# A fused linear-attention and ELU-MLP kernel on one core: filler on constant data in the opening, narrower W_in pieces, another bank for one slice, and the first q load ahead of the iota

## The chip, the core and the metric

The kernel runs on one core of a Trainium2 chip. The core has TensorE (PE, with its weight loads shown as PEld), VectorE (DVE), ScalarE (ACT), GpSimd (POOL) and SyncE (SP). The metric is the device time of one execution in microseconds (us); the time before is the median of eight runs. Lower is better.

## The reference

Two stages follow each other. The first is causal linear attention with a decay `lam` per head, over 4 batches, 8 heads, 768 positions and a head dimension of 64, in blocks of positions with a state carried from block to block:

```python
intra = einsum('bhij,bhjd->bhid', (qb @ kb.T) * Dmask, vb)   # Dmask = lam ** (i - j), i >= j
inter = einsum('bhid,bhde->bhie', qb * lam_pow, kv_state)
out[:, :, block] = intra + inter
kv_state = lam_block * kv_state + einsum('bhsd,bhse->bhde', kb_decayed, vb)
```

The second takes the result as `x`, 3072 tokens of 512 values, and computes

```python
h = x @ w_in                                       # 512 -> 2048
g = where(h > 0, h, exp(min(h, 0)) - 1)            # ELU
out = g @ w_out                                    # 2048 -> 512
```

## The kernel before, in words

**Groups and token tiles.** The kernel works with blocks of 128 positions. A group `g` is one block of one batch: 6 blocks by 4 batches make 24 groups, and groups 0 to 3 are the first block of each batch. The 24 groups are put together to token tiles `t` of 4, 2, 4, 4, 4, 4 and 2 groups (`TS`), so tile 0 is groups 0 to 3 with 512 tokens.

**Attention of a group.** q and k are transposed (`att_T`, lines 207 to 224, by TensorE with an identity as the other operand, into tiles `psTq`, `psTk` or `psT`; later groups by a DMA, `att_xT`) and copied to SBUF (`att_Te`, ScalarE). `att_S` makes the scores (`psS`), `att_mask` multiplies them by the decay mask (VectorE, L320), `att_O` multiplies by v and adds the part that comes from the state (`psO`), and `att_X` writes the result to `xt`. `att_kd` (L295) makes the decayed k, for groups 0 to 3 on GpSimd; `att_U` and `att_st` update the state.

**The MLP of a token tile.** W_in is cut into 16 slices of 128 columns. `mm1` multiplies slice `n` of W_in (L441, or L459 for the tiles of two groups) with `xt` into a PSUM tile `psH`. ScalarE takes its exp (`e`, L470) and its relu (`r`, L474), and VectorE joins them to `g` (L487). For slices 2, 4 and 6 of tile 0 there is no relu and VectorE does two steps (L482, L485). `mm2` (L538) multiplies `g` by W_out into `psM`, which is copied out and stored. The last group's output is made in two parts (`mm2_last`).

**PSUM.** There are three tags, "S", "M" and "H", with two buffers each. A tile with a tag waits for the readers of the tile two before it with the same tag. `psH` has the tag "H", but in tile 0 the even slices below 8 have "M", which `psM` and the filler also use.

**Order.** Nothing is scheduled by a planner: the order of the program on each engine is written out by hand in the list `steps` and in `run`, which hangs functions on steps. Steps `('A', n)` are slice `n` of tile 0; steps `('B', n)` are the rest of the second matmul of tile 0, in between which group 4's transposes stand (step `('B', 1)`). From step `(1, 0)` on, token tile 1 and later ones follow.

**Loads.** All loads of q, k, v, W_in and W_out convert from float32 to float16 and are issued by GpSimd (POOL) in the order of the list `LOADS`, L72 for q, k and v, L97 for W_in (`emit_wi`), L104 for W_out (`emit_wo`). Entries `(g, n, 'q')` load `n` groups; `('wi', i)` and `('wo', i)` load piece `i`; `('kd', g)` is no load but the computation of the decayed k on GpSimd, at this place of its order. The pieces have the widths of `WI = [1, 1, 2, 2, 2, 4, 4]` slices and `WO = [2, 2, 4, 4, 4]`. The first twelve entries are q and k of groups 0 to 3, then v; W_in follows. From the entry that loads group 8 on, loads hang on steps and are paced (`paced_load`) by a one-element copy on GpSimd that reads a finished `g`. The small load of `lam` is on SyncE.

**The opening.** GpSimd makes `rel_i` by an iota (L127) before the first load. From it VectorE makes `rel`, the identity `ident16` (L140), the causal mask, `pos`, `row` and the lag, and clears the states `st` (L156). ScalarE makes `loglam`, `dn`, and the masks (`build_mask0`, L170). Meanwhile `warm(k)` (L560 to 568) lets TensorE run `k` filler matmuls into a PSUM tile `psW` that nobody reads; their operand on both sides is `ident16`. The list `W` says how many stand ahead of each step of the opening: `W[0]` ahead of group 0's q transposes, `W[1]` ahead of its k transposes, and so on to the first slice of the MLP.

The code that the change touches:

Of the kernel before, what the change touches and what calls it, by code (L numbers as in the profile page):

```python
# [8 lines left out]
FP16 = mybir.dt.float16  # L9
# [6 lines left out]
def kernel(  # L16
# [27 lines left out]
    cpool = ctx.enter_context(tc.tile_pool(name="cst", bufs=1))  # L44
# [16 lines left out]
    def emit_load(g, n=1, which="qkv"):  # L61
        c, b = divmod(g, B)
        rows = slice(c * L, (c + 1) * L)
        i, o = (g // 2) % NB, (g % 2) * H
        for w, src in (("q", q), ("k", k), ("v", v)):
            if w not in which:
                continue
            if w == "v":
                dst = vn[i][:, o : o + n * H, :]
            else:  # L70
                dst = (qn if w == "q" else kn)[i][:, o : o + n * H, :]
            nc.gpsimd.dma_start(  # L72
                out=dst, in_=src[b : b + n, :, rows].rearrange("b h p d -> p (b h) d")
            )
# [7 lines left out]

    WI = [1, 1, 2, 2, 2, 4, 4]
    WO = [2, 2, 4, 4, 4]
    wi_t, wo_t, wi_at, wo_at = [], [], {}, {}
    for i, w in enumerate(WI):
        for j in range(w):
# [7 lines left out]
    def emit_wi(i):  # L95
        f0 = sum(WI[:i]) * 128
        nc.gpsimd.dma_start(  # L97
            out=wi_t[i][:],
            in_=moe_w_in[:, f0 : f0 + WI[i] * 128].rearrange("(k p) f -> p k f", p=128),
        )  # L100

    def emit_wo(i):
        f0 = sum(WO[:i]) * 128
        nc.gpsimd.dma_start(  # L104
            out=wo_t[i][:],
            in_=moe_w_out[f0 : f0 + WO[i] * 128, :].rearrange("(n p) f -> p n f", p=128),
        )
# [4 lines left out]
    ]  # L112
    LOADS = [(0, 1, 'q'), (0, 1, 'k'), (1, 1, 'q'), (1, 1, 'k'), (2, 1, 'q'), (2, 1, 'k'), (3, 1, 'q'), (3, 1, 'k'), (0, 1, 'v'), (1, 1, 'v'), (2, 1, 'v'), (3, 1, 'v'), ('wi', 0), ('wi', 1), ('wi', 2), ('wi', 3), ('kd', 0), ('wi', 4), ('wi', 5), ('kd', 2), ('wo', 0), ('wi', 6), ('wo', 1), ('wo', 2), (4, 2), ('wo', 3), ('wo', 4), (6, 2), (8, 2), (10, 2), (12, 2), (14, 2), (16, 2), (18, 2), (20, 2), (22, 2)]

    def run_loads(items):
        for it in items:
            if it[0] == "wi":
                emit_wi(it[1])
            elif it[0] == "wo":
                emit_wo(it[1])  # L120
            elif it[0] == "kd":
                att_kd(it[1], 2, "p")
            else:
                emit_load(*it)

    run_loads(LOADS[:0])
    nc.gpsimd.iota(rel_i[:], pattern=[[1, 128]], base=0, channel_multiplier=-1)  # L127
    run_loads(LOADS[0:16])

# [6 lines left out]
    ident16 = cpool.tile([128, 128], FP16, name="ident16")  # L136
# [47 lines left out]
    def late_ks():  # L184
        nc.scalar.activation(ks[:], loglam[:], AF.Exp, scale=pos[:, 1:2])
# [15 lines left out]
    qT, kT, Pt, kds, xt, pT, pS = {}, {}, {}, {}, {}, {}, {}  # L201
# [230 lines left out]
    def mm1_mm(t, n, lo, hi, tag="H"):  # L432

        if n == 0 and lo == 0:
            gt[t] = msb.tile([128, NF, TS[t] * L], FP16, tag="g", bufs=2, name=f"g{t}")
        if lo == 0:
            pH_of[t, n] = ps.tile([128, TS[t] * L], FP32, tag=tag, bufs=2, name=f"psH{t}_{n}")
        pH = pH_of[t, n]
        wi, j = wi_t[wi_at[n][0]], wi_at[n][1]
        for kk in range(HP):  # L440
            nc.tensor.matmul(  # L441
                pH[:, lo:hi], lhsT=wi[:, kk, j * 128 : (j + 1) * 128],
                rhs=xt[t][:, kk, lo:hi], start=(kk == 0), stop=(kk == HP - 1),
            )

    def mm1(t, n, alt=False):

        MT = TS[t] * L
        if MT == 256:
            if n == 0:  # L450
                gt[t] = msb.tile([128, NF, MT], FP16, tag="g", bufs=2, name=f"g{t}")
            pH = ps.tile(
                [128, 2 * MT], FP32, tag="M" if (t, n) in ((1, 0),) else "H", bufs=2,
                name=f"psH{t}_{n}",
            )
            for x in range(2):
                wi, j = wi_t[wi_at[n + x][0]], wi_at[n + x][1]
                for kk in range(HP):
                    nc.tensor.matmul(  # L459
                        pH[:, x * MT : (x + 1) * MT],  # L460
                        lhsT=wi[:, kk, j * 128 : (j + 1) * 128],
                        rhs=xt[t][:, kk, :], start=(kk == 0), stop=(kk == HP - 1),
                    )
            MT *= 2
        else:
            if (t, n) not in pH_of:
                mm1_mm(t, n, 0, MT, "M" if t == 0 and n % 2 == 0 and n < 8 else "H")
            pH = pH_of.pop((t, n))
        e = msb.tile([128, MT], FP32, tag="e", bufs=3, name=f"e{t}_{n}")
        nc.scalar.activation(e[:], pH[:], AF.Exp)  # L470
        if alt:
            return e, None, pH
        r = msb.tile([128, MT], FP16, tag="r", bufs=3, name=f"r{t}_{n}")
        nc.scalar.activation(r[:], pH[:], AF.Relu)  # L474
        return e, r, pH
# [84 lines left out]
    def warm(k, tag="M"):  # L560
        if k <= 0:
            return
        pw = ps.tile([128, 4, 128], FP32, tag=tag, bufs=2, name=f"psW{len(warms)}")
        warms.append(pw)
        for _ in range(k):
            nc.tensor.matmul(  # L566
                pw[:, 0:2], lhsT=ident16[:], rhs=any16[:, 0:2], start=True, stop=True
            )

    warms = []  # L570
    pace = cpool.tile([1, 1], FP16, name="pace")
    any16 = ident16[:].unsqueeze(1).broadcast_to([128, 4, 128])

# [33 lines left out]
    op_T(2, "q")  # L607
    op_Te(2, "q")
    att_S(1)
    att_mask(1, 2)  # L610
    warm(W[5])
    op_T(2, "k")
# [31 lines left out]

    run_loads(LOADS[16:28])
    for s, g in zip([], (0, 2)):
# [35 lines left out]
    def paced_load(s, items):  # L682

        t, n = s
        if t not in ("A", "B"):
            w = 2 if TS[t] == 2 else 1
            src = gt[t][0:1, n - w, 0:1] if n else gt[t - 1][0:1, NF - 1, 0:1]
            nc.gpsimd.tensor_copy(pace[:], src)  # L688
        run_loads(items)

    for s, a, b in [(('B', 2), 28, 29), ((1, 2), 29, 30), ((1, 14), 30, 31), ((2, 4), 31, 32), ((2, 12), 32, 33), ((3, 4), 33, 34), ((3, 12), 34, 35), ((4, 4), 35, 36)]:
        at(s, paced_load, s, LOADS[a:b])

    steps = [(('A', 0), (0, 0), []), (('A', 1), (0, 1), []), (('A', 2), (0, 2), []), (('A', 3), (0, 3), []), (('A', 4), (0, 4), []), (('A', 5), (0, 5), []), (('A', 6), (0, 6), []), (('A', 7), (0, 7), []), (('A', 8), (0, 8), []), (('A', 9), (0, 9), []), (('A', 10), (0, 10), [(0, 0, 0), (0, 1, 0)]), (('A', 11), (0, 11), [(0, 0, 1), (0, 1, 1)]), (('A', 12), (0, 12), [(0, 0, 2), (0, 1, 2)]), (('A', 13), (0, 13), [(0, 0, 3), (0, 1, 3)]), (('A', 14), (0, 14), [(0, 0, 4), (0, 1, 4)]), (('A', 15), (0, 15), [(0, 0, 5), (0, 1, 5)]), (('B', 0), None, [(0, 2, 0), (0, 2, 1), (0, 2, 2), (0, 2, 3)]), (('B', 1), None, [(0, 2, 4), (0, 2, 5), (0, 3, 0), (0, 3, 1)]), (('B', 2), None, [(0, 3, 2), (0, 3, 3), (0, 3, 4), (0, 3, 5)]), (('B', 3), None, [(0, 0, 6), (0, 1, 6), (0, 2, 6), (0, 3, 6)]), (('B', 4), None, [(0, 0, 7), (0, 1, 7), (0, 2, 7), (0, 3, 7)]), (('B', 5), None, [(0, 0, 8), (0, 1, 8), (0, 2, 8), (0, 3, 8)]), (('B', 6), None, [(0, 0, 9), (0, 1, 9), (0, 2, 9), (0, 3, 9)]), (('B', 7), None, [(0, 0, 10), (0, 1, 10), (0, 2, 10), (0, 3, 10)]), (('B', 8), None, [(0, 0, 11), (0, 1, 11), (0, 2, 11), (0, 3, 11)]), (('B', 9), None, [(0, 0, 12), (0, 1, 12), (0, 0, 13), (0, 1, 13)]), (('B', 10), None, [(0, 0, 14), (0, 1, 14), (0, 0, 15), (0, 1, 15)]), (('B', 11), None, [(0, 2, 12), (0, 3, 12), (0, 2, 13), (0, 3, 13)]), (('B', 12), None, [(0, 2, 14), (0, 3, 14), (0, 2, 15), (0, 3, 15)]), ((1, 0), (1, 0), []), ((1, 2), (1, 2), []), ((1, 4), (1, 4), []), ((1, 6), (1, 6), [(1, 0, 0), (1, 1, 0), (1, 0, 1), (1, 1, 1)]), ((1, 8), (1, 8), [(1, 0, 2), (1, 1, 2), (1, 0, 3), (1, 1, 3)]), ((1, 10), (1, 10), [(1, 0, 4), (1, 1, 4), (1, 0, 5), (1, 1, 5)]), ((1, 12), (1, 12), [(1, 0, 6), (1, 1, 6), (1, 0, 7), (1, 1, 7)]), ((1, 14), (1, 14), [(1, 0, 8), (1, 1, 8), (1, 0, 9), (1, 1, 9)]), ((2, 0), (2, 0), [(1, 0, 10), (1, 0, 11)]), ((2, 1), (2, 1), [(1, 0, 12), (1, 0, 13)]), ((2, 2), (2, 2), [(1, 0, 14), (1, 0, 15), (1, 1, 10)]), ((2, 3), (2, 3), [(1, 1, 11), (1, 1, 12)]), ((2, 4), (2, 4), [(1, 1, 13), (1, 1, 14)]), ((2, 5), (2, 5), [(1, 1, 15), (2, 0, 0), (2, 0, 1)]), ((2, 6), (2, 6), [(2, 0, 2), (2, 0, 3)]), ((2, 7), (2, 7), [(2, 0, 4)]), ((2, 8), (2, 8), [(2, 0, 5), (2, 1, 0)]), ((2, 9), (2, 9), [(2, 0, 6), (2, 1, 1)]), ((2, 10), (2, 10), [(2, 0, 7), (2, 1, 2)]), ((2, 11), (2, 11), [(2, 0, 8), (2, 1, 3)]), ((2, 12), (2, 12), [(2, 0, 9), (2, 1, 4)]), ((2, 13), (2, 13), [(2, 0, 10), (2, 1, 5)]), ((2, 14), (2, 14), [(2, 0, 11), (2, 1, 6)]), ((2, 15), (2, 15), [(2, 0, 12), (2, 1, 7)]), ((3, 0), (3, 0), [(2, 0, 13), (2, 1, 8), (2, 0, 14), (2, 1, 9)]), ((3, 1), (3, 1), [(2, 0, 15), (2, 1, 10), (2, 1, 11), (2, 1, 12)]), ((3, 2), (3, 2), [(2, 1, 13), (2, 1, 14), (2, 1, 15), (2, 2, 0)]), ((3, 3), (3, 3), [(2, 2, 1), (2, 2, 2), (2, 2, 3), (2, 2, 4), (2, 2, 5)]), ((3, 4), (3, 4), [(2, 2, 6), (2, 2, 7), (2, 2, 8), (2, 2, 9)]), ((3, 5), (3, 5), [(2, 2, 10), (2, 2, 11), (2, 2, 12), (2, 2, 13)]), ((3, 6), (3, 6), [(2, 2, 14), (2, 2, 15), (2, 3, 0), (2, 3, 1), (2, 3, 2)]), ((3, 7), (3, 7), [(2, 3, 3), (2, 3, 4), (2, 3, 5), (2, 3, 6)]), ((3, 8), (3, 8), [(2, 3, 7), (2, 3, 8), (2, 3, 9), (2, 3, 10)]), ((3, 9), (3, 9), [(2, 3, 11), (2, 3, 12), (2, 3, 13), (2, 3, 14), (2, 3, 15)]), ((3, 10), (3, 10), [(3, 0, 0), (3, 0, 1), (3, 0, 2), (3, 0, 3)]), ((3, 11), (3, 11), [(3, 0, 4), (3, 0, 5), (3, 1, 0), (3, 0, 6)]), ((3, 12), (3, 12), [(3, 1, 1), (3, 0, 7), (3, 1, 2), (3, 0, 8), (3, 1, 3)]), ((3, 13), (3, 13), [(3, 0, 9), (3, 1, 4), (3, 0, 10), (3, 1, 5)]), ((3, 14), (3, 14), [(3, 0, 11), (3, 1, 6)]), ((3, 15), (3, 15), [(3, 0, 12), (3, 1, 7)]), ((4, 0), (4, 0), [(3, 0, 13), (3, 1, 8), (3, 0, 14), (3, 1, 9)]), ((4, 1), (4, 1), [(3, 0, 15), (3, 1, 10), (3, 1, 11), (3, 1, 12)]), ((4, 2), (4, 2), [(3, 1, 13), (3, 1, 14), (3, 1, 15), (3, 2, 0)]), ((4, 3), (4, 3), [(3, 2, 1), (3, 2, 2), (3, 2, 3), (3, 2, 4), (3, 2, 5)]), ((4, 4), (4, 4), [(3, 2, 6), (3, 2, 7), (3, 2, 8), (3, 2, 9)]), ((4, 5), (4, 5), [(3, 2, 10), (3, 2, 11), (3, 2, 12), (3, 2, 13)]), ((4, 6), (4, 6), [(3, 2, 14), (3, 2, 15), (3, 3, 0), (3, 3, 1), (3, 3, 2)]), ((4, 7), (4, 7), [(3, 3, 3), (3, 3, 4), (3, 3, 5), (3, 3, 6)]), ((4, 8), (4, 8), [(3, 3, 7), (3, 3, 8), (3, 3, 9), (3, 3, 10)]), ((4, 9), (4, 9), [(3, 3, 11), (3, 3, 12), (3, 3, 13), (3, 3, 14), (3, 3, 15)]), ((4, 10), (4, 10), [(4, 0, 0), (4, 0, 1), (4, 0, 2), (4, 0, 3)]), ((4, 11), (4, 11), [(4, 0, 4), (4, 0, 5), (4, 1, 0), (4, 0, 6)]), ((4, 12), (4, 12), [(4, 1, 1), (4, 0, 7), (4, 1, 2), (4, 0, 8), (4, 1, 3)]), ((4, 13), (4, 13), [(4, 0, 9), (4, 1, 4), (4, 0, 10), (4, 1, 5)]), ((4, 14), (4, 14), [(4, 0, 11), (4, 1, 6)]), ((4, 15), (4, 15), [(4, 0, 12), (4, 1, 7)]), ((5, 0), (5, 0), [(4, 0, 13), (4, 1, 8), (4, 0, 14), (4, 1, 9)]), ((5, 1), (5, 1), [(4, 0, 15), (4, 1, 10), (4, 1, 11), (4, 1, 12)]), ((5, 2), (5, 2), [(4, 1, 13), (4, 1, 14), (4, 1, 15), (4, 2, 0)]), ((5, 3), (5, 3), [(4, 2, 1), (4, 2, 2), (4, 2, 3), (4, 2, 4), (4, 2, 5)]), ((5, 4), (5, 4), [(4, 2, 6), (4, 2, 7), (4, 2, 8), (4, 2, 9)]), ((5, 5), (5, 5), [(4, 2, 10), (4, 2, 11), (4, 2, 12), (4, 2, 13)]), ((5, 6), (5, 6), [(4, 2, 14), (4, 2, 15), (4, 3, 0), (4, 3, 1), (4, 3, 2)]), ((5, 7), (5, 7), [(4, 3, 3), (4, 3, 4), (4, 3, 5), (4, 3, 6)]), ((5, 8), (5, 8), [(4, 3, 7), (4, 3, 8), (4, 3, 9), (4, 3, 10)]), ((5, 9), (5, 9), [(4, 3, 11), (4, 3, 12), (4, 3, 13), (4, 3, 14), (4, 3, 15)]), ((5, 10), (5, 10), [(5, 0, 0), (5, 0, 1), (5, 0, 2), (5, 0, 3)]), ((5, 11), (5, 11), [(5, 0, 4), (5, 0, 5), (5, 1, 0), (5, 0, 6)]), ((5, 12), (5, 12), [(5, 1, 1), (5, 0, 7), (5, 1, 2), (5, 0, 8), (5, 1, 3)]), ((5, 13), (5, 13), [(5, 0, 9), (5, 1, 4), (5, 0, 10), (5, 1, 5)]), ((5, 14), (5, 14), [(5, 0, 11), (5, 1, 6)]), ((5, 15), (5, 15), [(5, 0, 12), (5, 1, 7)]), ((6, 0), (6, 0), [(5, 0, 13), (5, 1, 8), (5, 0, 14), (5, 1, 9), (5, 0, 15)]), ((6, 2), (6, 2), [(5, 1, 10), (5, 1, 11), (5, 1, 12), (5, 1, 13), (5, 1, 14)]), ((6, 4), (6, 4), [(5, 1, 15), (5, 2, 0), (5, 2, 1), (5, 2, 2), (5, 2, 3), (5, 2, 4)]), ((6, 6), (6, 6), [(5, 2, 5), (5, 2, 6), (5, 2, 7), (5, 2, 8), (5, 2, 9)]), ((6, 8), (6, 8), [(5, 2, 10), (5, 2, 11), (5, 2, 12), (5, 2, 13), (5, 2, 14)]), ((6, 10), (6, 10), [(5, 2, 15), (5, 3, 0), (5, 3, 1), (5, 3, 2), (5, 3, 3), (5, 3, 4)]), ((6, 12), (6, 12), [(5, 3, 5), (5, 3, 6), (5, 3, 7), (5, 3, 8), (5, 3, 9)]), ((6, 14), (6, 14), [(5, 3, 10), (5, 3, 11), (5, 3, 12), (5, 3, 13), (5, 3, 14), (5, 3, 15)]), (('E', 0), None, [(6, 0, 0), (6, 0, 1), (6, 0, 2), (6, 0, 3), (6, 0, 4), (6, 0, 5), (6, 0, 6), (6, 0, 7), (6, 0, 8), (6, 0, 9), (6, 0, 10), (6, 0, 11), (6, 0, 12), (6, 0, 13), (6, 0, 14), (6, 0, 15), (6, 1, 0), (6, 1, 1), (6, 1, 2), (6, 1, 3), (6, 1, 4), (6, 1, 5), (6, 1, 6), (6, 1, 7), (6, 1, 8), (6, 1, 9), (6, 1, 10), (6, 1, 11), (6, 1, 12), (6, 1, 13), (6, 1, 14), (6, 1, 15)])]
    for s, m1, m2 in steps:
        er = None
        if m1 is not None:
            t, n = m1
# [46 lines left out]
```

## Time and profile before

| what | before |
|---|---|
| median of 8 runs | 212.86 us |
| lowest and highest run | 212.38 and 213.5 us |
| the profiled execution's own time | 213.5 us |
| span of the profiled execution | 211.7 us |
| TensorE busy | 203.1 us, 96% of the span |
| VectorE, ScalarE, GpSimd busy | 148.5, 128.4 and 61.5 us |
| chain that ended last, by engine | PE 75%, POOL 11%, DMA 6%, DVE 3%, ACT 2% |
| load queue of GpSimd | 80384 packets, 14.16 MB |

The profile shows one execution. Its span runs from the first to the last instruction on the engines. A line of the timeline gives the start, the duration, the engine, the source line, the operation with its output and inputs, and how many instructions are merged; in brackets is the idle time of that engine just before, and what ended it. L-numbers are lines of the kernel before. Buffer numbers are left out of tile names, so `kn` is any buffer that holds k.

### The profile page before, as it was taken

How to read it: one execution, taken by the hardware profiler on the slowest of the kernel's cores; microseconds unless marked ns; L12 is line 12 of the kernel's file. 1: busy time of each engine (PE TensorE's matmuls, PEld its weight loads, DVE VectorE, ACT ScalarE, POOL GpSimd, SP SyncE). 2: the span in 40 equal slices, each digit the busy share in tenths (PEclk: the TensorE clock that was granted, in tenths of full speed). 3: DMA queues.
4: the chain of work that ended last, by engine and by line, in shares of the span. 5: the costliest groups of instructions: out<-in, count | busy, mean ns of one | idle time of the engine just before them, and what ended most of it. 6: DMA issues, size and time to landing. Idle time of an engine off the chain costs nothing.

```text
span 211.7 us, 4157 instructions
## 1 busy us (share of the span) xinstructions
PE 203.1 (96%) x1654; PEld 107.2 (51%) x1654; DVE 148.5 (70%) x240; ACT 128.4 (61%) x247; POOL 61.5 (29%) x70
## 2 busy tenths in 40 slices
PE   5997999999999999999999999999999999999994
PEld 3653444556765454544544544544544544466643
DVE  6774996477989999998698598677557634344321
ACT  6886888305784858666464566464567476675620
POOL 8999963600333251150600510600000000011000
PEclk9999999999999999999999999999999999999999
DMA  6999999999999999999699891599401111011112
GB/s 39 142 156 170 180 201 165 200 157 185 194 156 154 136 170 160 132 96 107 114 140 159 106 130 53 111 147 155 85 0 53 50 50 50 5 50 50 50 53 101
DMA packets 100756, 24.40 MB, mean 115 GB/s; under 512 B 93056, under 2 KB 97920, under 8 KB 100736
## 3 DMA queue, kind: packets, MB, share of 16 engines
q0 software_dynamic: 80384, 14.16, 87.5%
q1 hardware_dynamic: 20208, 9.90, 21.5%
q8 instruction: 13, 0.21, 0.4%
q10 hardware_dynamic: 144, 0.07, 0.1%
q14 instruction: 7, 0.06, 0.1%
HBM read 27.27 MB, written 6.29 MB: 158 GB/s over the span
## 4 chain that ended last, share of the span: by engine, by line
PE 75%; POOL 11%; DMA 6%; DVE 3%; ACT 2%; issue 1%; POOLq 0%; ACTq 0%
PE psM L538 34%; PE psH L441 26%; DMA kn<-in_k_dram 6%; PE psH L459 5%; POOL wi L97 2%; PE psO L334 2%; PE psS L308 2%; POOL qn L72 2%; PE psO L342 2%; POOL kd L295 2%; POOL kn L72 2%; PE psM L518 2%; POOL vn L72 2%; DVE g L487 1%; DVE P L320 1%; ACT kd L293 1%
## 5 line engine op out<-in xcount | busy, mean ns | idle before, releaser
L538 PE MATMUL psM<-wo,g 128*128 128x512 f16 x368 | 94.0, 380 | 0.2 <-DVE g L487 0.2
L470 ACT ACTIVATE e<-psH 128x512 f32<-128x512 f32 x96 | 57.3, 597 | 59.9 <-PE psH L441 50.7
L487 DVE SCALAR_TENSOR_TENSOR g<-e,r 128x512 f16<-128x512 f32 x93 | 64.2, 702 | 37.5 <-ACT r L474 37.2
L441 PE MATMUL psH<-xt,wi 128*128 128x512 f16 (+2 forms) x324 | 81.5, 377 | 1.9 <-DMA wi<-in_moe_w_in_dram 1.5
L474 ACT ACTIVATE r<-psH 128x512 f16<-128x512 f32 x93 | 55.1, 593 | 0.0
L538 PEld LDWEIGHTS <-g 128*128 128x128 f16 x368 | 34.2, 98 | 38.6 <-DVE g L487 1.5
L441 PEld LDWEIGHTS <-wi 128*128 128x128 f16 x324 | 31.1, 98 | 39.9 <-DMA wi<-in_moe_w_in_dram 2.1
L320 DVE TENSOR_TENSOR P<-psS,mask 128x1024 f16<-128x1024 f32 (+1 forms) x28 | 28.7, 1066 | 5.4 <-PE psS L308 5.3
L688 POOL COPY pace<-g 1x1 f16<-1x1 f16 x7 | 2.3, 329 | 68.5 <-DVE g L487 68.5
L418 DVE SCALAR_TENSOR_TENSOR st<-st,up_p,psU 64x128 f16<-64x128 f16 x64 | 18.2, 345 | 0.1
L555 POOL DMA_DIRECT2D out_dram<-osb x2 | 1.1, 570 | 54.8 <-ACT osb L554 50.7
L72 POOL DMA_DIRECT2D qn<-in_q_dram x14 | 15.3, 1091 | 5.8 <-issue 2.0
L363 DVE TENSOR_TENSOR xt<-psO,qs 128x1024 f16<-128x1024 f32 x10 | 12.2, 1223 | 6.7 <-PE psO L342 6.7
L459 PE MATMUL psH<-xt,wi 128*128 128x256 f16 x128 | 16.5, 273 | 0.0
L72 POOL DMA_DIRECT2D vn<-in_v_dram x14 | 15.2, 1105 | 2.3 <-DMA wo<-in_moe_w_out_dram 2.0
L72 POOL DMA_DIRECT2D kn<-in_k_dram x14 | 15.2, 1089 | 0.1
L554 ACT COPY osb<-psM 128x512 f32<-128x512 f32 x12 | 7.1, 592 | 12.2 <-PE psM L538 12.2
L459 PEld LDWEIGHTS <-wi 128*128 128x128 f16 x128 | 12.3, 98 | 4.2
L334 PEld LDWEIGHTS <-vn 128*64 128x64 f16 x184 | 9.6, 110 | 4.8 <-issue 3.8
L334 PE MATMUL psO<-P,vn 128*64 128x128 f16 x184 | 11.5, 222 | 0.3 <-DMA vn<-in_v_dram 0.2
L342 PE MATMUL psO<-qT,st 128*64 128x128 f16 x160 | 10.0, 219 | 0.0
L566 PE MATMUL psW<-ident 128*128 128x256 f16 x34 | 8.0, 360 | 1.6 <-DVE ident L140 1.6
(58 smaller groups left out, 118.2 us busy)
## 6 DMA issues: line engine op xcount, KB each, us to landing
out_dram<-osb SPq DMA_DIRECT2D x21, 256.0 KB, 2.3
qn<-in_q_dram POOLq DMA_DIRECT2D x10, 256.0 KB, 6.9
kn<-in_k_dram POOLq DMA_DIRECT2D x10, 256.0 KB, 7.6
vn<-in_v_dram POOLq DMA_DIRECT2D x10, 256.0 KB, 9.6
wo<-in_moe_w_out_dram POOLq DMA_DIRECT2D x3, 512.0 KB, 15.6
wi<-in_moe_w_in_dram POOLq DMA_DIRECT2D x2, 512.0 KB, 8.5
wi<-in_moe_w_in_dram POOLq DMA_DIRECT2D x3, 256.0 KB, 6.7
qn<-in_q_dram POOLq DMA_DIRECT2D x4, 128.0 KB, 4.4
```

The lines of the kernel that those rows point to most:

```text
L72: nc.gpsimd.dma_start(out=dst, in_=src[b : b + n, :, rows].rearrange("b h p d -> p (b h) d"))
L320: nc.vector.tensor_tensor(out=P[:, :, c], in0=s[:, :, c], in1=(mask if g < B else mask1)[:, :, c], op=ALU.mult,)
L334: nc.tensor.matmul(po[r, i, hp, :], lhsT=v_of(g + i, 2 * hp + hh), rhs=P[:, hh, hp, :], start=True, stop=(c == 0), skip_group_check=True,)
L342: nc.tensor.matmul(po[r, i, hp, :], lhsT=st[(g + i) % B // 2][c % 2][:, (g + i) % 2, hp, r], rhs=qT[g + i][:, hp, :], start=False, stop=Tr ...
L363: nc.vector.tensor_tensor(out=dst, in0=po[:, :, c], in1=qs[:, c].unsqueeze(1).broadcast_to([128, n, w, 128]), op=ALU.mult,)
L418: nc.vector.scalar_tensor_tensor(out=new[r, :, hp, r], in0=old[r, :, hp, r], scalar=up_p[r, hp : hp + 1], in1=pu[r, :, hp, :], op0=ALU.mul ...
L441: nc.tensor.matmul(pH[:, lo:hi], lhsT=wi[:, kk, j * 128 : (j + 1) * 128], rhs=xt[t][:, kk, lo:hi], start=(kk == 0), stop=(kk == HP - 1),)
L459: nc.tensor.matmul(pH[:, x * MT : (x + 1) * MT], lhsT=wi[:, kk, j * 128 : (j + 1) * 128], rhs=xt[t][:, kk, :], start=(kk == 0), stop=(kk = ...
L470: nc.scalar.activation(e[:], pH[:], AF.Exp)
L474: nc.scalar.activation(r[:], pH[:], AF.Relu)
L487: nc.vector.scalar_tensor_tensor(out=g, in0=e[:], scalar=-1.0, in1=r[:], op0=ALU.add, op1=ALU.min)
L538: nc.tensor.matmul(pm[:], lhsT=gt[t][:, n, i * L : (i + 1) * L], rhs=wo_t[wo_at[n][0]][:, wo_at[n][1], :], start=(n == 0), stop=(n == NF - 1),
```

## The change

The change has four parts, and one branch more.

1. A tile `ones` of 128x128 in float16 is set to 1.0 by VectorE as its first instruction. The filler matmuls read it on both sides instead of `ident16`, and `W` has other numbers, 52 fillers in all instead of 34.
2. `WI` becomes `[1, 1, 2, 2, 2, 2, 2, 4]`: slices 8 to 11 are loaded as two pieces of two slices. In `LOADS` the second of them comes after `('kd', 2)` and ahead of W_out's piece 0; the ranges of `LOADS` that later steps issue move by one.
3. Slice 8 of tile 0 takes its PSUM tile from the tag "M" instead of "H".
4. The first load, q of group 0, is issued by GpSimd ahead of the iota instead of behind it.
5. `paced_load` has a branch for steps of `A` and `B`, which holds if group 6's decayed k has been made by then.

```diff
+    ones = cpool.tile([128, 128], FP16, name="ones")
+    nc.vector.memset(ones[:], 1.0)
...
-    WI = [1, 1, 2, 2, 2, 4, 4]
+    WI = [1, 1, 2, 2, 2, 2, 2, 4]
...
-    LOADS = [... ('kd', 0), ('wi', 4), ('wi', 5), ('kd', 2), ('wo', 0), ('wi', 6), ('wo', 1), ('wo', 2), (4, 2), ...]
+    LOADS = [... ('kd', 0), ('wi', 4), ('wi', 5), ('kd', 2), ('wi', 6), ('wo', 0), ('wi', 7), ('wo', 1), ('wo', 2), (4, 2), ...]
...
-    run_loads(LOADS[:0])
+    run_loads(LOADS[:1])
     nc.gpsimd.iota(rel_i[:], pattern=[[1, 128]], base=0, channel_multiplier=-1)
-    run_loads(LOADS[0:16])
+    run_loads(LOADS[1:16])
...
-                mm1_mm(t, n, 0, MT, "M" if t == 0 and n % 2 == 0 and n < 8 else "H")
+                mm1_mm(t, n, 0, MT, "M" if t == 0 and n % 2 == 0 and n < 9 else "H")
...
-                pw[:, 0:2], lhsT=ident16[:], rhs=any16[:, 0:2], start=True, stop=True
+                pw[:, 0:2], lhsT=ones[:], rhs=any16[:, 0:2], start=True, stop=True
...
-    any16 = ident16[:].unsqueeze(1).broadcast_to([128, 4, 128])
+    any16 = ones[:].unsqueeze(1).broadcast_to([128, 4, 128])
...
-    W = [10, 4, 3, 1, 2, 1, 2, 1, 3, 0, 0, 2, 0, 2, 0, 0, 3, 0, 0, 0]
+    W = [18, 7, 3, 2, 3, 1, 2, 2, 4, 0, 0, 3, 0, 3, 0, 0, 4, 0, 0, 0]
...
-    run_loads(LOADS[16:28])
+    run_loads(LOADS[16:29])
...
             nc.gpsimd.tensor_copy(pace[:], src)
+        elif 6 in kds:
+            nc.gpsimd.tensor_copy(pace[:], kds[6][0:1, 0, 0:1])
         run_loads(items)
```

More of the change, by code (lines that the diff above doesn't have):

```diff
@@ L112 @@
     ]
-    LOADS = [(0, 1, 'q'), (0, 1, 'k'), (1, 1, 'q'), (1, 1, 'k'), (2, 1, 'q'), (2, 1, 'k'), (3, 1, 'q'), (3, 1, 'k'), (0, 1, 'v'), (1, 1, 'v'), (2, 1, 'v'), (3, 1, 'v'), ('wi', 0), ('wi', 1), ('wi', 2), ('wi', 3), ('kd', 0), ('wi', 4), ('wi', 5), ('kd', 2), ('wo', 0), ('wi', 6), ('wo', 1), ('wo', 2), (4, 2), ('wo', 3), ('wo', 4), (6, 2), (8, 2), (10, 2), (12, 2), (14, 2), (16, 2), (18, 2), (20, 2), (22, 2)]
+    LOADS = [(0, 1, 'q'), (0, 1, 'k'), (1, 1, 'q'), (1, 1, 'k'), (2, 1, 'q'), (2, 1, 'k'), (3, 1, 'q'), (3, 1, 'k'), (0, 1, 'v'), (1, 1, 'v'), (2, 1, 'v'), (3, 1, 'v'), ('wi', 0), ('wi', 1), ('wi', 2), ('wi', 3), ('kd', 0), ('wi', 4), ('wi', 5), ('kd', 2), ('wi', 6), ('wo', 0), ('wi', 7), ('wo', 1), ('wo', 2), (4, 2), ('wo', 3), ('wo', 4), (6, 2), (8, 2), (10, 2), (12, 2), (14, 2), (16, 2), (18, 2), (20, 2), (22, 2)]
     def run_loads(items):
@@ L688, in paced_load @@
             nc.gpsimd.tensor_copy(pace[:], src)
+        elif 6 in kds:
+            nc.gpsimd.tensor_copy(pace[:], kds[6][0:1, 0, 0:1])
         run_loads(items)
-    for s, a, b in [(('B', 2), 28, 29), ((1, 2), 29, 30), ((1, 14), 30, 31), ((2, 4), 31, 32), ((2, 12), 32, 33), ((3, 4), 33, 34), ((3, 12), 34, 35), ((4, 4), 35, 36)]:
+    for s, a, b in [(('B', 2), 29, 30), ((1, 2), 30, 31), ((1, 14), 31, 32), ((2, 4), 32, 33), ((2, 12), 33, 34), ((3, 4), 34, 35), ((3, 12), 35, 36), ((4, 4), 36, 37)]:
         at(s, paced_load, s, LOADS[a:b])
```

## The prediction

> **What bounds the kernel now.** I read the page first: TensorE is busy 96% of the span, so what can be won lies in its few idle places and in what stands before them. The list of TensorE's waits comes next (us in total, times, longest):
>
> ```profile
> PE psW L566 <- DVE ident L140: 1.6, 1, 1.6
> PE psH L441 <- DMA wi<-in_moe_w_in_dram: 1.5, 2, 1.3
> PE psTq L221 <- DMA qn<-in_q_dram: 0.9, 1, 0.9
> PE psH L441 <- ACT r L474: 0.3, 1, 0.3
> ...
> PE psT L221 <- DMA kn<-in_k_dram: 0.3, 1, 0.3
> ```
>
> All lie before 39 us. An idle place is worth something only if no later wait takes the time back, so the last one decides. The chain that ended last, in order of time (start, us, what):
>
> ```profile
> 1.39 1.05 POOL qn L72
> 2.44 0.90 POOL kn L72
> ...
> 24.37 13.65 DMA kn<-in_k_dram
> 38.07 0.62 PE psT L221 x8
> 38.69 2.59 PE psM L538 x12
> ```
>
> Up to 24.37 the chain is GpSimd (POOL) issuing loads, then it is one transfer, the k of groups 4 and 5, until 38.07. From there it is nearly all TensorE to the end: in 100 to 212 us TensorE is busy 108.8 us, and what is left is mostly the last eviction and store. So the time is the landing of that k, plus a fixed rest of about 174 us.
>
> Why does that k take 13.65 us, when the first q took 3.5? Because loads queue. The stage table (columns: busy time of five engines, clock, DMA share, GB/s), asked for a stretch in which two-slice W_in pieces flow and one in which four-slice W_in and W_out pieces flow:
>
> ```profile
> 16.90:18.90 2.00, 0.81 (x7) 0.35 (x5) 0.18 (x2) 1.46 (x4) 2.00 (x4) 1.00 1.36 181
> 24.50:30.50 6.00, 5.69 (x42) 2.50 (x40) 5.84 (x11) 5.09 (x10) 4.19 (x5) 1.00 1.24 204
> ```
>
> The page's DMA row shows 9 in nearly every slice from 5 us to 95 us: the queue never empties for long, so its end is where it starts plus what is carried. The timeline has TensorE's side of the meeting point and the opening:
>
> ```profile
> 0.84 0.23 POOL L127 IOTA rel_i<- 128x128 int32 x1 [0.39 <-POOLq L729]
> ...
> 1.65 2.31 PE L566 MATMUL psW<-ident 128*128 128x256 f16 x10 [1.65 <-DVE ident L140]
> ...
> 19.01 1.04 PE L441 MATMUL psH<-xt,wi 128*128 128x512 f16 x4 [1.31 <-DMA wi<-in_moe_w_in_dram]
> ...
> 28.55 1.02 PE L441 MATMUL psH<-xt,wi 128*128 128x512 f16 x4 [0.31 <-ACT r L474]
> ```
>
> **The sum's footing.** The profiled execution took 213.5 us for a span of 211.7, 1.8 outside it. It was the slowest of the eight; the median is 212.86. I add differences to the median and come back to the 0.64.
>
> **Filler on ones.** It adds one 128x128 fp16 memset on VectorE (nearest row: four 128x512 memsets in 2.11 us, so under 0.53; bound below 0) and takes the identity out of the filler's way. VectorE idles until 1.11, so the memset hides. Filler can start near 1.0 instead of 1.65, and there are 52 filler matmuls instead of 34. Before 10.4 us a filler takes 0.231 (10 in 2.31), later about 0.11 apart. 18 slow ones end near 1.0 + 18 x 0.231 = 5.2, and the first q transposes (4.90 before) go 0.3 late; seven more (1.6) could put the first k's transposes at 5.2 + 0.6 + 1.6 = 7.4 against 6.65, and the ScalarE copy of it (7.85, behind its masks) about 0.2 late. If the filler brings the fast clock early, the slow transposes (four in 0.61) become 0.39 and nothing is late. Both die out: TensorE waits for the q load of group 3 at 11.58, for v loads at 13.50 to 16.16, and then 1.31 for W_in piece 1 at 19.01. The five extra fillers behind 11.58 cost about 0.11 each, 0.55 in all, inside the 1.31. On the path: 0.
>
> This row I weigh against the Trainium skill, "TensorE: Matmul & The Clock Gate", Part 1: about 3.4 us of sustained activity releases a gate that halves the clock. The trace agrees in kind (filler mean 421 ns to 9.8 us, 273 ns from 10.9). By the rule the filler would release the clock around 5 us and halve some 4 us of slow TensorE work, an estimated 2 us of gain taken alone, and the sum would be 210.8; by the rows of waits it is 0.
>
> **First q ahead of the iota.** The first q is issued near 0.8 instead of 1.39. That q gains about 0.6, and nobody needs it: the copy of it on ScalarE starts at 6.21 behind the masks. The iota moves behind it, by 1.05, and so do the rel, identity, causal and position steps on VectorE. Their block (1.11 to 4.89) then ends at 5.94; the three mask steps (1.29, 0.68, 0.69) end at 8.6; the first masked score at 9.13 stays put, with 0.5 over. ScalarE's dn (4.83) and mask (5.04) need position and lag by 3.0 and 3.8. On GpSimd what counts is the second load, k of group 0, since every later load queues behind it. Before it came iota, a 0.32 gap and 1.05 of q issue; now the same three in another order: 2.44 again. Bounds: 0.3 earlier if the gap between a small compute step and a DMA issue goes (copies ahead of DMA issues show up to 0.4), 0.3 later if the first DMA of the program has such a gap of its own. I take 0, as the same pieces add up. On the path: 0, from -0.3 to +0.3.
>
> **Two-slice pieces.** W_in's slices 8 to 11 come as two loads, the second behind the second kd on GpSimd, and W_out piece 0 moves one place back. No bytes are added; one issue (0.8) is. That issue pushes W_out 0, the last W_in piece, W_out 1 and 2 and the loads of groups 4 and 5 back by 0.8 at GpSimd. The k is then issued near 25.2 and lands near 38, so the queue hides the 0.8; without that queue it would cost all of it. GpSimd also waits, with eight loads outstanding, for the oldest to land (q of group 6 at 29.98, after 1.81 of waiting on W_in). One load more moves this by one place: q of group 4 then waits for piece 3, k for piece 4; they landed at 21.1 and 22.8 (issue plus time to landing, from the list of DMA issues asked by stretch; so are all landings here), before their turn. What remains is the rate: 512 KiB as narrower rows, 0.524 MB at 181 GB/s is 2.90 us, at 204 it is 2.57: +0.33. The other bound is from landings: two-slice pieces landed 1.2, 1.0 and 1.7 after the load ahead, mean 1.3, so 2.6 for two, while the four-slice piece landed 3.1 after the one ahead: -0.5. Both rows are of this very queue, so I take their middle, -0.1.
>
> The skill's "DMA: Bandwidth & Descriptors", section Anatomy of one DMA, speaks against this edit: each DMA carries about 2.0 us of fixed cost, so a split would add 2.0 and give some 214.9. Here landings 1.0 to 1.7 apart show such a cost overlapped.
>
> **Third bank for slice 8.** Slice 8 goes to the other pair of banks, so slice 10 no longer waits for slice 8's relu: the 0.31 at 28.55 goes. What is late next: VectorE works without a break from 28.36 to 32.97, and slice 13 needs slice 11's relu (31.66 + 0.59 = 32.25) against its start at 32.43. So 0.18 to 0.31 reaches the transposes at 37.18. There the q of group 4 landed at 37.0 and the k at 38.07: TensorE arrives earlier and waits longer. On the path: 0. The new branch in the paced loads issues nothing: group 6's decayed k is not made yet when it is asked for.
>
> **Sum.** 0 + 0 - 0.1 + 0 = -0.1 on 212.86: 212.8.
>
> **Rivals.** *TensorE's saving is paid out (faster).* If the k lands earlier, by an earlier second load or by pieces that cost less, TensorE gains the 0.28 it waits there and its own 0.18 to 0.31, 0.46 to 0.59; with 0.3 from the opening's W_in wait moving along, at most 0.89. For it: the median run is 0.64 quicker than the profiled one, so in a typical run that k may land earlier than 38.07 and TensorE be nearer to the bound. Against: the queue is full and the bytes are the same. Time: 212.86 - 0.59 = 212.3. What is late next would be the k of group 6: landed 48.5, wanted at 49.63, 1.1 spare.
>
> *The stream gets later (slower).* One mechanism: the k of group 4 lands late because the second load is issued behind the iota and the narrow rows then flow at 181 GB/s. Price up to 0.3 + 0.33 = 0.63: 213.5. It decides as soon as the k lands after 38.07, every 0.1 costing 0.1, since TensorE executes in order behind those transposes.
>
> *It does nothing that can be told* is the likeliest case, with its own range of 212.45 to 213.25: 0.2% (0.43 us) is about what a measurement of this kernel can tell from no change.
>
> **How the numbers follow.** Chances: 0.42 for the likeliest, 0.34 for the faster rival, 0.24 for the slower. The faster one is ahead of the slower because the filler and bank edits only take waits away. The range runs from 212.86 - 0.89 = 212.0 to 212.86 + 0.63 = 213.5.
>
> **What would show it.** Filler from about 1 us, the second load at 2.44 give or take 0.3, no TensorE wait on relu for slice 10, W_in waits near 19 us as before, and a wait on k of group 4 grown from 0.28 to about 0.5, ending near 38.0. If that wait is gone and the transposes start before 37.5, the faster rival holds; if it ends after 38.4, the slower. I am wrong in kind if the time moves while that k lands where it did, or if new idle time shows on TensorE after 40 us.

## The result, and the profile after

The changed kernel takes 213.67 us (median of 12 runs, 213.15 to 214.13) against 212.90 for the kernel before (33 runs). The ratio is 1.0034 with a 95% interval of 1.0026 to 1.0043: 0.77 us slower, outside the predicted range of 212.0 to 213.5. The profiled execution took 213.94 us for a span of 212.2.

TensorE's waits in the changed kernel, the same list as before (us in total, times, longest):

```profile
PE psH L443 <- DMA wi<-in_moe_w_in_dram: 1.5, 2, 1.3
PE psW L568 <- DVE ones L55: 1.1, 1, 1.1
...
PE psT L223 <- DMA kn<-in_k_dram: 0.6, 1, 0.6
```

No wait for slice 8's relu is left, the filler starts 0.6 us earlier (1.06 instead of 1.65), and the wait on the k of group 4 has doubled, from 0.28 to 0.56. The chain that ended last turns on that same load:

```profile
12.26 2.97 POOL wi L99 x4
15.23 1.93 POOL kd L297
17.16 1.43 POOL wi L99 x2
18.59 1.93 POOL kd L297
20.52 0.69 POOL wi L99
...
25.37 13.06 DMA kn<-in_k_dram
38.43 0.05 issue
38.48 0.62 PE psT L223 x8
```

`POOL kd` is the computation of the decayed k on GpSimd. The chain of the kernel before has it at the same places:

```profile
15.05 1.93 POOL kd L295
16.98 1.43 POOL wi L97 x2
18.41 1.93 POOL kd L295
20.34 0.64 POOL wo L104
```

The k lands at 38.43 instead of 38.07. What follows is as long as before: from the start of its transposes to the end of the span it was 173.66 us before (211.73 - 38.07) and 173.68 after. This holds in all eighteen kernels of this study, from 173.60 to 173.69, although the start itself moves from 36.84 to 38.76. In ten of their profiles the transposes wait for that k; in the other eight they start without such a wait. So the whole change lies ahead of 38.5 us, and one number tells of it: when TensorE starts the k transposes of group 4. The profiled execution of before was the slowest of the first eight. By the median, its transposes start near 212.90 - 1.8 - 173.65 = 37.45, those of the changed kernel near 38.2. Each profile is one execution, up to 0.8 us from the median of its kernel, and its waits and rates are to be read with that in mind.

The stage table of the changed kernel for three stretches, and then that of before (last column: GB/s of all transfers):

```profile
20.00:23.00 3.00, 2.65 (x13) 1.24 (x14) 2.59 (x4) 1.55 (x4) 3.00 (x5) 1.00 1.35 172
23.00:26.00 3.00, 3.00 (x29) 1.27 (x27) 2.76 (x6) 2.54 (x5) 3.00 (x4) 1.00 1.11 150
26.00:30.00 4.00, 4.00 (x33) 1.90 (x33) 3.91 (x7) 3.53 (x8) 3.19 (x4) 1.00 1.21 192
```

```profile
20.00:23.00 3.00, 2.85 (x14) 1.28 (x14) 2.65 (x4) 2.54 (x5) 3.00 (x5) 1.00 1.23 164
23.00:26.00 3.00, 3.00 (x30) 1.26 (x30) 2.76 (x6) 2.40 (x5) 3.00 (x4) 1.00 1.14 181
26.00:30.00 4.00, 3.69 (x32) 1.77 (x32) 3.91 (x7) 3.54 (x7) 2.19 (x4) 1.00 1.24 205
```

From 23 to 26 us the loads move at 150 GB/s instead of 181, and from 26 to 30 us at 192 instead of 205. That is where the stream falls behind in these two profiles; the experiments ask why.

### The profile page after: what moved, and what is told of

It reads as the page before. It is cut to its first block, busy times and chain, and to the rows that moved or that the text cites. A ratio compares the mean times of both kernels' runs of the same rounds, so it can differ in the third digit from the quotient of the medians.

```text
span 212.2 us, 4194 instructions
## 1 busy us (share of the span) xinstructions
PE 203.4 (96%) x1672; PEld 107.8 (51%) x1672; DVE 148.5 (70%) x241; ACT 128.1 (60%) x247; POOL 62.3 (29%) x71
## 4 chain that ended last, share of the span: by engine, by line
PE 75%; POOL 11%; DMA 6%; DVE 3%; ACT 2%; issue 1%; POOLq 0%; ACTq 0%
PE psM L540 34%; PE psH L443 26%; DMA kn<-in_k_dram 6%; PE psH L461 5%; POOL wi L99 3%; PE psO L336 2%; PE psS L310 2%; POOL qn L74 2%; PE psO L344 2%; POOL kd L297 2%; PE psM L520 2%; POOL vn L74 2%; POOL kn L74 2%; DVE g L489 1%; DVE P L322 1%
## 5 line engine op out<-in xcount | busy, mean ns | idle before, releaser
L568 PE MATMUL psW<-ones 128*128 128x256 f16 x52 | 9.3, 317 | 1.1 <-DVE ones L55 1.1
```

## The experiments

**One part undone at a time.** Theory A: the load stream sets the time. Theory B: TensorE's added filler does. Theory C: the other order of banks does. The diffs are shortened to the parts of a line that change; ranges of `LOADS` that move along are left out.

`a1_wide`, the changed kernel with W_in's pieces as before:

```diff
-    WI = [1, 1, 2, 2, 2, 2, 2, 4]
+    WI = [1, 1, 2, 2, 2, 4, 4]
-  ('kd', 2), ('wi', 6), ('wo', 0), ('wi', 7), ('wo', 1)
+  ('kd', 2), ('wo', 0), ('wi', 6), ('wo', 1)
```

> The changed kernel with slices 8 to 11 as one four-slice load again, everything else as changed. Theory A, the load stream sets the time: the k of group 4 lands about 0.2 to 0.3 us earlier than in the changed kernel (38.2 instead of 38.43), the wait of TensorE on it falls from 0.56 to about 0.3, and the time falls by 0.2 to 0.4 us, to a ratio near 1.0020 of the kernel before. Theory B, TensorE's own added work in the opening (18 more fillers) sets it: no change, ratio 1.0034.

Measured: 1.0000 (0.9988 to 1.0013), 213.03 us. In its profile, of an execution 0.61 us quicker than the median, the transposes start at 37.02 without any wait on the load. The gain was larger than expected, the whole loss.

`a2_iota_first`, the changed kernel with the iota ahead of the first load:

```diff
-    run_loads(LOADS[:1])
+    run_loads(LOADS[:0])
     nc.gpsimd.iota(...)
-    run_loads(LOADS[1:16])
+    run_loads(LOADS[0:16])
```

> The changed kernel with the iota ahead of the first q load again. Theory A: the second load is issued at 2.44 instead of 2.60, the group 0 v load 0.19 earlier as in the kernel before, the k of group 4 lands some 0.19 us earlier and the time falls by 0.2 us, to a ratio near 1.0025. Theory B: no change, 1.0034.

Measured: 1.0026 (1.0016 to 1.0036). The second load is issued at 2.43 instead of 2.60, as expected; the time is in the expected direction, but its interval overlaps that of the changed kernel.

`a3_bank8`, the changed kernel with slice 8 on "H":

```diff
-    "M" if t == 0 and n % 2 == 0 and n < 9 else "H"
+    "M" if t == 0 and n % 2 == 0 and n < 8 else "H"
```

> The changed kernel with slice 8 back on the tag H. Theory A: slice 10 waits about 0.3 us for slice 8's relu again, TensorE reaches the k transposes of group 4 a little later and waits less for the load; no change of time, ratio 1.0034. A third theory C, that the other order of banks costs time: the time falls to that of the kernel before.

Measured: 1.0031 (1.0019 to 1.0042), the same as the changed kernel. Theory C falls.

`a4_filler_old`, the changed kernel with the old filler:

```diff
-    W = [18, 7, 3, 2, 3, 1, 2, 2, 4, 0, 0, 3, 0, 3, 0, 0, 4, 0, 0, 0]
+    W = [10, 4, 3, 1, 2, 1, 2, 1, 3, 0, 0, 2, 0, 2, 0, 0, 3, 0, 0, 0]
...
-    lhsT=ones[:]
+    lhsT=ident16[:]
...
-    any16 = ones[:]
+    any16 = ident16[:]
```

> The changed kernel with the old filler: the identity as operand and 34 fillers. Theory A: TensorE starts slow again and catches up at the q load of group 3; no change of time, ratio 1.0034. Theory B, that the added filler delays TensorE in the opening: the time falls by 0.5 us or more, to a ratio of 1.0010 or less.

Measured: 1.0051 (1.0036 to 1.0065), 213.97 us. Theory B falls with its sign reversed: without the new filler the kernel is, if anything, slower. With the iota late, the old filler waits 3.6 us for the identity instead of 1.6, so this run prices the old filler together with a late identity.

**One part alone, on the kernel before.** The edits are the reverse of those above.

> The kernel before with only the first q load ahead of the iota. Theory A, the load stream sets the time: the second load is issued at 2.60 instead of 2.44, every later one 0.19 later, the k of group 4 lands near 38.25 instead of 38.07 and the time rises by 0.2 us, ratio 1.0009. Theory B, only TensorE's own added work counts: ratio 1.0000.

Measured: 1.0008 (0.9991 to 1.0025). The second load at 2.58 instead of 2.44; the time is too close to be told from no change. In its profile the k transposes start at 37.63 and wait for nothing, so the late landing near 38.25 that theory A expected is not seen there.

> The kernel before with only W_in's slices 8 to 11 as two loads of two slices, in the changed order. Theory A: narrower rows move at a lower rate and the k of group 4 lands 0.2 to 0.35 us later; the time rises by that, ratio 1.0010 to 1.0016. Theory B: 1.0000.

Measured: 1.0034 (1.0021 to 1.0048), 0.72 us: the whole loss, from this one edit, and twice what theory A expected of it. The second load is issued at 2.43, so nothing ahead of W_in has moved; the transposes start at 38.47 after a wait of 0.67.

> The kernel before with only the filler on ones and its larger counts. Theory A: TensorE's clock is granted about 6 us earlier, and nothing later moves, as the q load of group 3 and the W_in pieces are awaited as before; ratio 1.0000. Theory B: the 18 more fillers delay TensorE, ratio 1.0025 to 1.0034.

Measured: 0.9987 (0.9965 to 1.0008), unresolved, on the faster side.

> The kernel before with only slice 8 on the tag M. Theory A: the 0.31 us wait of slice 10 goes and the wait on the k of group 4 grows by as much; ratio 1.0000. Theory C, that the other order of banks costs time: ratio 1.002 or more.

Measured: 1.0011 (0.9997 to 1.0025), too close to be told from no change. In its profile slice 10 follows slice 9 without a wait, and the wait on the k of group 4 is 0.81: what TensorE saved it waited.

The four singles add up to +0.0040 against the measured 0.0034, so nothing needs an interaction.

**Why do two-slice pieces cost 0.7 us?** They differ in three ways: the rows are narrower (N), half of the bytes are issued behind the second decayed-k computation on GpSimd, which takes 2.0 us during which no load is issued (G), and there is one load more to issue. The expectations below leave the third out; with it the k of group 4 is issued at 25.05 instead of 24.37. GpSimd's timeline in `b2_narrow`:

```profile
16.78 1.62 POOL L97 DMA_DIRECT2D wi<-in_moe_w_in_dram  x2
18.34 1.99 POOL L295 TENSOR_TENSOR kd<-kn,ks 128x1024 f16<-128x1024 f16 x1
20.19 0.83 POOL L97 DMA_DIRECT2D wi<-in_moe_w_in_dram  x1
```

The two loads at 16.78 are 512 KiB together; in the kernel before the same two are 768 KiB.

`d1_narrow_early` issues both narrow loads ahead of the computation:

```diff
-  ('wi', 5), ('kd', 2), ('wi', 6), ('wo', 0)
+  ('wi', 5), ('wi', 6), ('kd', 2), ('wo', 0)
```

> The kernel before with the two narrow loads of slices 8 to 11 both ahead of the second kd on GpSimd, so that the issue of them is not interrupted. Theory N, the narrow rows cost the time: the queue moves about 150 GB/s from 23 to 26 us as in the other narrow kernels, the k of group 4 lands near 38.5, ratio 1.003 or more. Theory G, the queue runs short because half of the bytes are issued only behind the 2 us of kd: the rate from 23 to 26 us is back near 180, ratio 1.0000 to 1.0010.

Measured: 1.0020 (1.0004 to 1.0035). The rate from 23 to 26 us is back at 176 GB/s, but from 20 to 23 it is 145: the computation now starts 0.8 later, and so does everything behind it. Between the two theories, so it does not decide between them. It issues one load more as well, with the halves side by side, and is slower by 0.43 us (0.09 to 0.75): the extra load may be a good part of the loss, and no run here prices it alone.

`d2_wide_late`, the kernel before with the wide load behind the computation:

```diff
-  ('wi', 4), ('wi', 5), ('kd', 2), ('wo', 0)
+  ('wi', 4), ('kd', 2), ('wi', 5), ('wo', 0)
```

> The kernel before with the four-slice load of slices 8 to 11 moved behind the second kd, rows as wide as before. Theory G: ahead of the kd only one two-slice load has been issued, so the queue runs short for longer than in the changed kernel; the k of group 4 lands 0.8 us or more later, ratio 1.004 or more. Theory N: no narrow rows, ratio 1.0000 to 1.0010.

Measured: 1.0070 (1.0042 to 1.0098), and 119 GB/s from 20 to 23 us. The price is G's, but not all of it is paid where G said: slice 8 waits 1.74 us for its own piece and starts at 27.42, and the k transposes at 38.76 wait for nothing.

```profile
27.42 1.90 PE L441 MATMUL psH<-xt,wi 128*128 128x512 f16 x8 [1.74 <-DMA wi<-in_moe_w_in_dram]
```

This kernel issues no load more than the kernel before, so a gap with too little issued ahead of it is enough to lower the rate and cost time.

`e3_wide_halves` has the changed kernel's order and bytes with wide rows. The four-slice piece is halved by rows of the contraction instead of by columns:

```diff
-    out=wi_t[i][:], in_=moe_w_in[:, f0 : f0 + w].rearrange("(k p) f -> p k f", p=128)
+    out=wi_t[i][:, half], in_=moe_w_in[:, f0 : f0 + w].rearrange("(k p) f -> p k f", p=128)[:, half]
-  ('wi', 5), ('kd', 2), ('wo', 0)
+  ('wi', (5, 0)), ('kd', 2), ('wi', (5, 1)), ('wo', 0)
```

> The kernel before with slices 8 to 11 loaded by two loads of 256 KiB, one ahead of and one behind the second kd as in the changed kernel, but halved by rows of the contraction, so that the rows are as wide as before. Theory G, the queue runs short behind the kd: the rate from 23 to 26 us falls to 150 to 165 GB/s, the k of group 4 lands near 38.4, ratio 1.0025 to 1.0040. Theory N, the narrow rows cost: the rate stays near 180, ratio 1.0000 to 1.0010.

Measured: 1.0033 (1.0018 to 1.0049), the full loss, with the rows of slices 8 to 11 as wide as before. Its stage table, and under it that of `b2_narrow`:

```profile
20.00:23.00 3.00, 3.00 (x30) 1.40 (x28) 2.96 (x5) 2.52 (x5) 3.00 (x5) 1.00 1.20 169
23.00:26.00 3.00, 3.00 (x29) 1.35 (x30) 2.95 (x6) 2.41 (x5) 3.00 (x4) 1.00 0.97 125
26.00:30.00 4.00, 3.69 (x18) 1.63 (x17) 3.89 (x8) 3.15 (x6) 2.95 (x5) 1.00 1.23 204
```

```profile
20.00:23.00 3.00, 3.00 (x15) 1.34 (x16) 2.62 (x5) 1.72 (x4) 3.00 (x5) 1.00 1.34 177
23.00:26.00 3.00, 3.00 (x43) 1.40 (x41) 2.97 (x5) 2.33 (x5) 3.00 (x4) 1.00 1.20 150
26.00:30.00 4.00, 3.69 (x26) 1.60 (x19) 3.91 (x7) 3.61 (x8) 2.89 (x4) 1.00 1.17 184
```

The rate falls to 125 GB/s from 23 to 26 us, below the 150 to 165 expected. Against the kernel before the three stretches move +15, -168 and -4 KB, 157 KB less by 30 us, which at 205 GB/s is 0.77 us; the same sum for `b2_narrow` (177, 150, 184) is 138 KB or 0.67 us. Both stand beside measured losses of 0.70 and 0.72, but so close a match is partly luck: the seven kernels that load W_in in the old order at this place (the kernel before, `a1_wide`, `b1_q_first`, `b3_filler`, `b4_bank`, `c1_wo_split` and `c3_best`) moved 1814 to 1929 KB in these 10 us, a spread worth 0.56 us. The shortfall itself is clear of that spread: `e3_wide_halves` moved 1698 KB, and the six kernels with narrow pieces in the changed order 1660 to 1734.

So narrow rows are not needed for the loss: issuing half of the bytes later is enough, by the gap and the one load more together, and how the 0.7 us divides between these two stays open. That narrow rows add something is not excluded: from 26 to 30 us the narrow kernels move 182 to 192 GB/s, where `e3_wide_halves` is back at 204. That the queue runs short is read from issue times and rates, since no view shows what it holds. The other reading, that computing on GpSimd slows the transfers meanwhile, does not fit: in `b2_narrow` they move at 183 and 188 GB/s from 18 to 19 and 19 to 20 us, while GpSimd computes, and the rate drops only some 3 us later.

`e4_kd_late` goes the other way, the kernel before with more queued ahead of the gap:

```diff
-  ('wi', 5), ('kd', 2), ('wo', 0), ('wi', 6)
+  ('wi', 5), ('wo', 0), ('kd', 2), ('wi', 6)
```

> The kernel before with the second kd on GpSimd moved one place back, behind the first W_out load. Theory G: 256 KiB more are in the queue when GpSimd leaves it alone for 2 us, so the queue keeps its rate, the k of group 4 lands 0.2 to 0.5 us earlier, and the time falls by up to what TensorE waits there, ratio 0.9980 to 0.9995. Theory N: ratio 1.0000.

Measured: 0.9996 (0.9984 to 1.0009), inconclusive on the time. The rate did what G says, 186 GB/s from 20 to 23 us where before had 164, but the k transposes start at 37.66, right behind those of q, and wait for no load: TensorE is late by itself.

**Is the loss paid only at that k?** `c1_wo_split` puts 256 KiB less ahead of it:

```diff
-    WO = [2, 2, 4, 4, 4]
+    WO = [2, 2, 2, 2, 4, 4]
-  ('wo', 2), (4, 2), ('wo', 3), ('wo', 4)
+  ('wo', 2), (4, 2), ('wo', 3), ('wo', 4), ('wo', 5)
```

> The kernel before with the four-slice W_out load ahead of group 4 cut into two of two slices (rows of the same width), the second one issued behind group 4's loads. 256 KiB less stand ahead of the k of group 4. Theory A, the start of its transposes plus 173.65 us is the span: it lands about 1.3 us earlier, the wait on it goes, and the time falls by what TensorE waits there, 0.2 to 0.5 us, ratio 0.9977 to 0.9990. If the landing of that k does not set the time: ratio 1.0000.

Measured: 0.9984 (0.9971 to 0.9997), 212.68 us, within what theory A expected. The transposes start at 36.84 and wait for nothing.

> The changed kernel with the W_out load ahead of group 4 cut into two, the second one behind group 4's loads. If the loss is paid only where TensorE waits for the k of group 4, that wait goes (256 KiB are worth 1.3 us, the loss is 0.75) and the time falls by 0.5 to 0.75 us against the changed kernel, ratio 0.9985 to 1.0005. If the narrow pieces cost TensorE something else too, it stays above 1.0020.

Measured: 1.0010 (0.9998 to 1.0021), 213.16 us. The fall of 0.51 against the changed kernel is at the edge of what was expected; the ratio is outside the range given with it. The wait on the k is gone, but the timeline of TensorE shows the next one:

```profile
31.56 1.04 PE L443 MATMUL psH<-xt,wi 128*128 128x512 f16 x4 [1.70 <-DMA wi<-in_moe_w_in_dram]
```

That is slice 12 waiting for the last W_in piece, which stands in the same queue behind the same gap. (This execution was 0.77 us slower than the median of its kernel, so a wait of 1.70 is more than a typical one.)

The fair comparison is with `c1_wo_split`, since the split makes the kernel before faster too. With the split the change costs 1.0010 / 0.9984, a ratio of 1.0026 or 0.55 us; without it, 1.0034. The difference is inside the intervals. So the loss is not paid only at that k: most of it is still there when the k transposes wait for nothing, and by the profile it is then paid at slice 12.

**A better version.** `c3_best` is the kernel before with filler on ones, slice 8 on "M" and the split W_out load; `e5_best` has the filler, the split and the second decayed k one place later.

> The kernel before with the filler on ones, slice 8 on the tag M and the W_out load split as in c1_wo_split, W_in pieces and first load as before. Theory A: with the load out of the way, what TensorE saves in the opening and at slice 10 is paid out: the k transposes of group 4 start near 36.5 instead of 37.5, ratio 0.995 to 0.997, and the filler and bank edits are worth more here than alone (0.9987 and 1.0011). If that load does not set the time, the parts add up to 0.9998.

Measured: 0.9984 (0.9971 to 0.9998), 212.53 us. No more than the split alone; the expectation was missed. In its profile, of an execution 0.38 us slower than the median, TensorE waits 1.37 us for a v load at 16.51 and 0.81 for W_in at 26.54.

> The kernel before with the filler on ones, the second kd one place later and the W_out load split. If the load of k of group 4 alone held back what the filler saves: ratio 0.9965 to 0.9980. If TensorE's own W_in and v waits in the opening are the next bound, which c3_best points to: 0.9980 to 0.9990, no better than c1_wo_split.

Measured: 0.9989 (0.9980 to 0.9999), 212.82 us, within the second range and no better than `c1_wo_split` alone. Its profile has waits of 0.57 us for a v load and 0.4 for W_in. That such waits on earlier loads are the next bound is a reading of two profiles, not tested.

## Why the prediction was wrong

**What held.** The end is the start of the k transposes of group 4 plus a fixed rest, in every kernel run. The prediction put the landing of the k in the place of that start, which holds only where TensorE waits for it. The saving at slice 10 was worth nothing that can be told, as worked out. The first q load ahead of the iota moved the second load from 2.44 to 2.60, inside the bounds of 0.3 either way; its time, +0.0008 alone and as much when it is undone, is not resolved. The long wait for W_in came at 20.35, not near 19 as foretold, with 1.34 us as before (1.31).

The doubled wait of 0.56 agrees with the foretold "about 0.5" by luck. It was to grow because TensorE arrives earlier. In the changed kernel's profile TensorE arrives at 37.92 (38.48 - 0.56), against 37.79 before, and the wait is longer because the k lands 0.36 later:

```profile
37.31 0.61 PE L223 MATMUL psT<-ident,qn 128*128 128x128 f16 x8
38.48 0.62 PE L223 MATMUL psT<-ident,kn 128*128 128x128 f16 x8 [0.56 <-DMA kn<-in_k_dram]
```

The slower rival, the stream getting later, is what happened, and its sign, a wait that ends after 38.4, came (38.43). Its mechanism was another: a later second load and the rate of narrow rows, priced at 0.63 at most against the 0.77 measured.

**The step that failed is the term for two-slice pieces**, taken as -0.1 between -0.5 and +0.33 and measured alone at +0.72 (0.45 to 1.02 by its interval). The prediction priced the bytes (a rate of 181 against 204 GB/s, and gaps between landings) and wrote that the queue hides the extra issue. It did name that the second half comes behind the decayed k, but gave that nothing, and it read the chain up to 24.37 as "GpSimd (POOL) issuing loads", though two decayed k of 1.93 us each stand in it, in which nothing is issued. The rate does not hold there. The kernel before already moves less from 20 to 25 us than after it:

```profile
20.00:25.00 5.00, 4.85 (x37) 2.21 (x37) 4.41 (x7) 4.34 (x8) 5.00 (x7) 1.00 1.17 166
25.00:30.00 5.00, 4.69 (x36) 2.10 (x35) 4.91 (x9) 4.14 (x8) 3.19 (x5) 1.00 1.24 205
```

In the kernel before 768 KiB are issued just ahead of those 2.0 us, and even so the rate falls to 164 GB/s from 20 to 23 us; with 512 KiB, and one load more to issue behind them, it falls to 150 from 23 to 26 us and the k lands later. `e3_wide_halves` shows the same loss with wide rows, so the order of issuing, which the term left out, is enough for it. The page's DMA row, mostly 9, was read as a full queue. It is the mean busy share of 16 transfer engines, and that hardly tells the two kernels apart: from 23 to 26 us the share is 1.11 at 150 GB/s and 1.14 at 181.

**Filler.** Taken as 0. Removing it from the changed kernel moves the ratio from 1.0034 to 1.0051, adding it to the kernel before gives 0.9987: both point to a gain of about 0.3 us, neither is clear of its interval. What it does is seen in the timeline, first of the changed kernel, then of the kernel before:

```profile
1.06 3.73 PE L568 MATMUL psW<-ones 128*128 128x256 f16 x18 [1.06 <-DVE ones L55]
...
4.77 0.40 PE L223 MATMUL psTq<-ident,qn 128*128 128x128 f16 x4
```

```profile
4.90 0.61 PE L221 MATMUL psTq<-ident,qn 128*128 128x128 f16 x4 [0.94 <-DMA qn<-in_q_dram]
...
9.20 0.64 PE L221 MATMUL psTk<-ident,kn 128*128 128x128 f16 x4
...
10.97 0.39 PE L221 MATMUL psTk<-ident,kn 128*128 128x128 f16 x4
```

Four transposes at 4.77 take 0.40 where they took 0.61 at 4.90 before. In the kernel before four transposes still took 0.64 at 9.20 and 0.39 only from 10.97. The trace's record of the granted clock has the full clock from 4.36 us on in the changed kernel, 3.3 us after its filler starts, and from 10.35 in the kernel before. The Trainium skill, "TensorE: Matmul & The Clock Gate", Part 1, puts the release at about 3.4 us of sustained activity, and the trace of the changed kernel agrees. It is not the same in each execution: in the eight profiled kernels with this filler, all starting it at 1.06, the full clock comes between 3.74 (`c2_after_wo_split`) and 7.09 (`a2_iota_first`). The 2 us of gain that the prediction estimated from that page, taken alone, did not come.

The other page of the Trainium skill, "DMA: Bandwidth & Descriptors", Anatomy of one DMA, spoke against splitting the load, by about 2.0 us of fixed cost for each DMA. That cost does not appear in the time: `d1_narrow_early`, with its halves issued one behind the other, is 0.43 us slower, and `b2_narrow`, with a decayed k between them, 0.72.

**The 0.64 between the profiled run and the median** was noted, as something in favour of the faster rival, and not carried into the sum. By the median the transposes of the kernel before start near 37.45, ahead even of TensorE's arrival at 37.79 in that profile. So the 0.28 of waiting there need not be what a typical execution waits; whether that changed the size of the loss is not shown.

## What to carry to other kernels

Here GpSimd both computes and issues loads, and it issued none during each decayed k of 2.0 us; what is queued ahead of such a computation has to last through it. Before cutting or moving a load, add up the bytes issued ahead of each gap and the issue time that a further load adds, and read the rate stretch by stretch rather than the busy share. Where a span is one start plus a fixed rest, the time of that start is the measure of every edit ahead of it. To learn whether a loss is paid at one wait, take that wait away from both kernels, not only from the slower one.

## What the runs showed of the hardware

- A `g` step on VectorE that started while GpSimd made a decayed k ended only behind it. In the kernel before the one at 18.86 took 2.04 us, where the median of the 93 such steps is 0.69, and ended at 20.90, 0.56 after the decayed k. In `d1_narrow_early`, where the decayed k starts at 19.11, the step at 18.53 took 0.69 and the one at 19.88 took 1.80 and ended at 21.68, again 0.56 after it. What this costs in time was not tested.
- A W_in load takes GpSimd 0.81 to 0.88 us to issue in the kernel before, at 128, 256 and 512 KB alike, so loading the same bytes in more pieces takes more of its time, and the 2.0 us of one decayed k are worth more than two such loads.
- The rate of the loads differs with what is in the queue: 152 GB/s from 8 to 15 us of the kernel before, while q, k and v flow in packets of 128 bytes by the trace; 172 from 20 to 23 us of the changed kernel, with packets of 512 bytes; and 205 from 26 to 30 us of the kernel before, with packets of 1024 bytes.
